# Pooled attention ahead of two expert layers: the corner maxima, their row transfers, the opening's units and the last additions are rearranged

## The chip, the core and the metric

The kernel runs on one core of a Trainium2 chip. Its five engines work side by side, each through its own queue in order: PE (TensorE, matmuls), DVE (VectorE), ACT (ScalarE), POOL (GpSimd) and SP (SyncE, which issues the DMA transfers). The metric is the device time of one execution in microseconds (us); a lower time is better.

## The reference

For each of 4 batches and 8 heads, 1152 rows of q, k and v of width 64 come in. Pairs of q rows are averaged, which leaves 576, and each of them attends to all 1152 rows of k and v. Then come two layers over the 2304 x 512 result, whose code the change leaves as it is.

```python
q_pool = q.reshape(B, H, S // 2, 2, D).mean(axis=3)
scores = scale * np.matmul(q_pool, k.transpose(0, 1, 3, 2))
scores = scores - np.max(scores, axis=-1, keepdims=True)
attn = np.exp(scores)
attn = attn / (np.sum(attn, axis=-1, keepdims=True) + 1e-09)
x = np.matmul(attn, v)                     # then heads side by side: 2304 x 512
h = x @ w_in;  x = (h - np.tanh(h)) @ w_out
h = x @ w2_in; x = (h * sigmoid(1.702 * h)) @ w2_out
```

## The kernel before

**Pairs and halves.** Two heads are handled together, one on partitions 0 to 63 and one on 64 to 127, so there are 16 *pairs* p. Each pair has two *halves* of 288 q columns: half h = 2p (the *even* half) and h = 2p + 1 (the *odd* half), 32 in all. The order of the work is written out by hand: `todo[h]` says in which order PE gets score tiles and maximum units, and `at(h, place, job)` hangs everything else on a place of a half ("start", "load", "pre", "gp", "end").

**A half on PE.** It has 9 *score tiles* S (`scores`, L357), each 8 matmuls of 64x288: three products of the high and low parts of q and k, and last `row` x `sel`, which subtracts the row maximum. ACT turns each tile into `pf` by an exponential (L360). After the ninth, `products` multiplies the nine `pf` by v (L381) and adds up the sums by matmuls with ones (L388), from `terms`: the chain `sum` of the first six `pf`, which POOL adds in five additions (L371, `KADD = 6`), and the last three `pf`. Then ACT takes the result from PSUM (L396).

**The maxima.** Between the score tiles stand *units* (`unit`): each multiplies a piece of q by k into a PSUM tile and VectorE takes its maximum (L313). Each pair has 11: units 0 to 5, 7 and 8 (128 q columns x 512 keys), unit 6 (the last 128 keys of all columns), and units 9 and 10, the *corners* (the last 64 columns, from `cq`). In the hand-written order "X" is a unit of the next pair, "R" its unit 6, and "C" a corner of the pair's own. `max_rows` puts the maxima together: part 0 after unit 6 for the first 384 columns, part 1 for the rest, with two small reduces (L321, L324) and one 64x2 minimum of two SBUF operands (L325). `send_rows` transposes (L334) and has SP send each piece into the tile `row` (L340). An odd half's score tiles need part 1 of their own pair, and the even half's need part 0 alone. Before, part 1 is put together after the even half's products: `if x == 0: max_rows(p, 1); send_rows(p, 1)` (L569 to L571).

**PSUM.** Score tiles, units and products share one pool of four buffers (`ps`), which go round in order; a new tile can start when the one four places earlier has been read, a unit by DVE and a score tile by ACT.

**What else DVE and POOL do there.** Per pair: `prep_ql` (L271, DVE), `recip` (L417 the sum of two halves' sums, L418 plus 1e-9, L420 the reciprocal), `normalise` (L437), one of the conversion steps of the weights (L128, L134, L141, L148); on POOL `prep_kl` (L284), `prep_qs` (L260), and the weights' low part (L156). SP issues the loads of v, q and k for later pairs and the sums' small DMAs (`sums`, L409).

**Opening and end.** Seven units of pair 0 come first, among matmuls that keep PE busy (`keep_warm`, tile `warm`). At the end the first block of the attention's result is split into two parts for the next layer (`split_x`, L106 on ACT and L107 on DVE), two columns in each of the last two halves. The first matmuls of the layers are L605.

Of the kernel before, what the change touches and what calls it, by code (L numbers as in the profile page):

```python
# [7 lines left out]
F32 = mybir.dt.float32  # L8
# [3 lines left out]
ALU = mybir.AluOpType  # L12
# [16 lines left out]
def tile_pooled_attention_two_moe(  # L29
# [11 lines left out]
    nc = tc.nc  # L41
    B, NPB, _, S = k.shape
# [3 lines left out]
    HB = SP // 2  # L46
    KT = S // 128
    QJ = SP // 64
    NPAIR = B * NPB
# [12 lines left out]
    wpool = ctx.enter_context(tc.tile_pool(name="wpool", bufs=1))  # L62
# [139 lines left out]
    def attention(ctx: ExitStack):  # L202
# [5 lines left out]
        KADD = 6  # L208
# [10 lines left out]
        mts = [[fixed(f"{nm}{i}", 32) for nm in ("mt", "m2", "m3")] for i in range(2)]  # L219
        corners = [ap.tile([128, 3 * QL], F32R, name=f"cq{i}") for i in range(2)]  # L220
        rows = [ap.tile([128, SP], F32R, name=f"row{i}") for i in range(2)]

        def constants():
            nc.gpsimd.memset(f32(sel[:]), 0.0)
            for r in sides:
                nc.gpsimd.memset(f32(sel[r.start:r.start + 1, :]), 1.0)
            nc.gpsimd.memset(ones, 1.0)
            for t in corners:
                nc.gpsimd.memset(f32(t[:]), 0.0)
            for t in rows:  # L230
                nc.gpsimd.memset(f32(t[:]), 0.0)
# [4 lines left out]

        def new_pair(p):
            mt, m2, m3 = mts[p % 2]
            pairs[p] = dict(mt=mt, m2=m2, m3=m3, cq=corners[p % 2], row=rows[p % 2])

        def load_q(p, x=slice(0, SP)):
            if p not in qraw:
# [72 lines left out]
        def max_rows(p, part):  # L315
            d = pairs[p]
            n = 6 if part == 0 else 2
            at = 0 if part == 0 else 6
            m = d["m2"] if part == 0 else d["m3"]
            mt = f32(d["mt"][:, 0:24]).rearrange("p (c j) -> p j c", c=3)  # L320
            nc.vector.tensor_reduce(m[:, 0:n], mt[:, at:at + n, :], AX.X, ALU.min)  # L321
            if part == 1:
                c = f32(d["mt"][:, 24:28]).rearrange("p (a s) -> p s a", a=2)
                nc.vector.tensor_reduce(m[:, 2:4], c, AX.X, ALU.min)  # L324
                nc.vector.tensor_tensor(  # L325
                    m[0:64, 2:4], f32(m[0:64, 2:4]), f32(m[64:128, 2:4]), op=ALU.min)

        def send_rows(p, part):
            d = pairs[p]
            n = 6 if part == 0 else 2  # L330
            at = 0 if part == 0 else 6
            m = d["m2"] if part == 0 else d["m3"]
            tt = ap.tile([128, 32], F32R, tag="tt", name="tt", bufs=2)
            nc.vector.transpose(f32(tt[:]), f32(m[:]))  # L334
            for c in range(n + 2 * part):
                j, s = divmod(at + c, 2)
                q0 = 128 * j
                w = min(128, SP - q0)
                row = f32(d["row"][64 * s:64 * s + 1, q0:q0 + w])
                nc.sync.dma_start(  # L340
                    out=row.rearrange("o (a i) -> o a i", i=32),
                    in_=f32(tt[c:c + 32 * (w // 32 - 1) + 1:32, :]))

# [19 lines left out]
        def add(p, x, t):  # L363
            new = probs[(2 * p + x) * KT + t]
            if t == 0:
                parts[p, x] = new
                return
            out = parts[p, x]
            if t == 1:
                out = ap.tile([128, 2, HB], F32, tag="sum", name="sum")  # L370
            nc.gpsimd.tensor_add(out, parts[p, x], new)  # L371
            parts[p, x] = out

        def products(p, x):
            acc = ps.tile([128, 2, 512], F32, tag="ps", name="acc")[:, :, 0:HB]
            chain = parts.pop((p, x))
            new = [probs.pop((2 * p + x) * KT + t) for t in range(KT)]
            for t in range(KT):
                for n in range(4):
                    s, h = divmod(n, 2)  # L380
                    nc.tensor.matmul(  # L381
                        acc[32 * n:32 * n + 32, 0], pairs[p]["v"][:, s, t, 32 * h:32 * h + 32],
                        new[t][:, s, :], start=(t == 0), stop=(t == KT - 1))
            terms = [chain, *new[KADD:]]
            for i in range(0, len(terms), 2):
                for n in range(4):
                    s, h = divmod(n, 2)
                    nc.tensor.matmul(  # L388
                        acc[32 * n:32 * n + 32, 1], ones, terms[i + h][:, s, :],
                        start=(i == 0), stop=(i + 2 >= len(terms)))  # L390
            xs = slice(HB * x, HB * x + HB)
            if p < NPAIR - 1:
                if x == 0:
                    w = ap.tile([128, 2, SP], F32, tag="u", name="u", bufs=2)
                    results[p] = w[:, 0], w[:, 1], w
                nc.scalar.activation(results[p][2][:, :, xs], acc, AF.Copy)  # L396
            else:
                if x == 0:
                    results[p] = (
                        wpool.tile([128, SP], F32, name="u"), ap.tile([128, SP], F32, name="us"))  # L400
                for n in range(2):
                    nc.scalar.activation(results[p][n][:, xs], acc[:, n], AF.Copy)

        def sums(p):
            us = results[p][1]
            s9 = wpool.tile([128, 2, QJ], F32, tag="s9", name="s9", bufs=2)
            for n in range(4):
                s, h = divmod(n, 2)
                nc.sync.dma_start(  # L409
                    out=s9[sides[s], h, :],  # L410
                    in_=us[32 * n:32 * n + 1, :].rearrange("o (p i) -> o p i", i=QJ))
            norm[p] = dict(s9=s9)

        def recip(p):
            s9 = norm[p]["s9"]
            r9 = wpool.tile([128, QJ], F32, tag="r9", name="r9", bufs=2)
            nc.vector.tensor_reduce(r9, s9.rearrange("p h i -> p i h"), AX.X, ALU.add)  # L417
            nc.vector.tensor_scalar(  # L418
                out=r9, in0=r9, scalar1=1.0, scalar2=1e-9, op0=ALU.mult, op1=ALU.add)
            nc.vector.reciprocal(r9, r9)  # L420
            rd = drpool.tile([128, QJ], F32, tag="rd", name="rd", bufs=2)
            nc.sync.dma_start(out=rd, in_=r9)
            norm[p]["rd"] = rd
# [19 lines left out]
        def at(h, when, fn, *args):  # L443
            jobs.setdefault((h, when), []).append(lambda: fn(*args))

        def do(h, when):
            for job in jobs.pop((h, when), ()):
                job()

        usual = "S S C S C S X S S S X S S X X", "S X S S S X S R S S S X S X"  # L450
        NH = 2 * NPAIR
        todo = {}
        for h in range(NH):
            seq = list(usual[h % 2].replace(" ", ""))
            own = [9, 10] if h % 2 == 0 else []
            if h == 0:
                seq, own = list("SXSXSCSCSXSXSXSXS"), [7, 8, 9, 10]
            if h >= NH - 2:
                seq = [t for t in seq if t in ("SC" if h % 2 == 0 else "S")]
            other = list(range(0, 4) if h % 2 == 0 else range(4, 9))  # L460
            todo[h] = []
            for t in seq:
                if t == "S":
                    todo[h].append(None)
                elif own:
                    todo[h].append((h // 2, own.pop(0)))
                else:
                    todo[h].append((h // 2 + 1, other.pop(0)))
            assert todo[h].count(None) == KT and not own
            assert not other or h >= NH - 2  # L470

        order = (("i", 0), ("i", 1), ("o", 0), ("i", 2), ("i", 3), ("o", 1), ("o", 2), ("o", 3))
        slots_at = [h for h in range(2, NH) for _ in range(1 if h < NH - 2 else 3)]
# [6 lines left out]
                at(h, "end", job)  # L480
            at(min(mine[-1] + 1, NH - 1), "pre" if mine[-1] < NH - 1 else "end", split)
        for c in range(NKC):
            at(NH - 2 + c // 2, "end", split_x, 0, [c], nc.vector)

        for p in range(NPAIR):
            h = 2 * p
# [16 lines left out]
                at(h - 3, "pre", prep_kh, p, 1)  # L503
                at(h - 3, "pre", prep_qh, p)

        warm = ps.tile([128, 2, 512], F32, tag="ps", name="warm")

        def keep_warm(n):
            for _ in range(n):
# [39 lines left out]
        for h in range(NH):  # L549
            p, x = divmod(h, 2)  # L550
            do(h, "start")
            g = h * KT
            t = 0
            for u in todo[h]:
                if u is None:
                    scores(g + t)
                    if t < KADD:
                        add(p, x, t)
                    t += 1
                    continue  # L560
                unit(*u)
                if u == (p + 1, 6):
                    max_rows(p + 1, 0)
                    send_rows(p + 1, 0)
            do(h, "load")
            do(h, "pre")
            do(h, "gp")
            products(p, x)
            if x == 0:  # L569
                max_rows(p, 1)  # L570
                send_rows(p, 1)  # L571
            do(h, "end")
        sums(NPAIR - 1)
        assert not jobs
# [241 lines left out]
```

## Time and profile before

| | us |
|---|---|
| median of 3 runs | 1238.87 (1238.57 to 1239.13) |
| the profiled execution | 1240.21 |
| its span, first to last instruction | 1238.4 |
| attention, first score tile to the first matmul of the layers | 17.42 to 430.50 |
| granted TensorE clock, mean | 0.997 |

The profiled execution's own time is 1.34 us above the median, and its span 1.81 us below its own time. The mean clock is a share of the upper level (2.4 GHz). Two views are read most: the timeline, which lists the instructions by start, with the idle time of the engine just before and what ended it in brackets, and the waits, which add up the idle time of an engine by the line that waited and what released it. A line "x72" holds 72 merged instructions, and its duration runs from the first start to the last end.

### The profile page before, as it was taken

The page shows a single profiled execution, that of the slowest core. Times are in us where ns is not written, and L with a number is a line of the kernel's source. Part 1 is how long each engine was busy: PE and PEld are TensorE (multiplying, and loading weights), DVE is VectorE, ACT ScalarE, POOL GpSimd, SP SyncE. Part 2 cuts the span into 40 slices and gives each one's busy share as a digit, 9 for nine tenths or more (in the row PEclk, how much of TensorE's full clock was granted, in tenths as well). Part 3 has the DMA queues.
Part 4 walks back from the last instruction along what each step waited for, and adds up shares of the span by engine and source line. Part 5 has one row for each costly group of instructions (what it writes and reads, how often), then busy time and mean ns, then how long its engine had stood idle before and what let it go on. Part 6 is the DMA issues. An engine that isn't in the chain of part 4 may idle for free.

```text
span 1238.4 us, 23152 instructions
## 1 busy us (share of the span) xinstructions
PE 1214.8 (98%) x9484; PEld 986.7 (80%) x9484; DVE 921.3 (74%) x1067; ACT 623.8 (50%) x914; POOL 479.4 (39%) x325
## 2 busy tenths in 40 slices
PE   9999999999999999999999999999999999999998
PEld 7676766767667697898898898898888888888887
DVE  6578878888888489999999999999435645554333
ACT  3555655656555487676656666656333222222211
POOL 5678777787777612333333333221101001100000
PEclk9999999999999999999999999999999999999999
DMA  4222322222321111111011111111101110110011
GB/s 154 78 78 86 103 108 89 78 87 90 122 87 41 29 44 35 52 51 52 34 40 46 35 51 35 34 52 67 37 34 51 51 35 34 52 35 18 26 56 72
DMA packets 30506, 73.09 MB, mean 59 GB/s; under 512 B 11200, under 2 KB 11712, under 8 KB 30400
## 3 DMA queue, kind: packets, MB, share of 16 engines
q1 hardware_dynamic: 30400, 71.62, 16.6%
q8 instruction: 74, 1.21, 0.4%
q14 instruction: 32, 0.26, 0.1%
HBM read 66.58 MB, written 4.79 MB: 58 GB/s over the span
## 4 chain that ended last, share of the span: by engine, by line
PE 66%; DVE 18%; ACT 6%; DMA 3%; SPq 2%; issue 2%; POOL 1%; DVEq 0%; POOLq 0%; ACTq 0%
PE y L700 23%; PE h L605 21%; PE sc L357 11%; PE acc L381 6%; DVE mt L313 3%; DVE gg L663 2%; DVE gg L646 2%; PE mx L301 2%; DVE wt L128 2%; ACT u L644 2%; DVE wt L134 2%; SPq L340 2%; DMA row<-tt 2%; ACT a L665 2%; PE acc L388 2%
## 5 line engine op out<-in xcount | busy, mean ns | idle before, releaser
L313 DVE TENSOR_REDUCE mt<-mx 128x2 fp32r<-128x1024 f32 (+2 forms) x176 | 195.6, 1137 | 71.4 <-PE mx L301 39.0
L605 PE MATMUL h<-hl,big 128*128 128x512 f32 (+1 forms) x940 | 213.5, 379 | 0.0
L156 POOL TENSOR_TENSOR big<-wt,big 128x512 fp32r<-128x512 f32 x46 | 60.5, 1316 | 367.7 <-ACT big L155 367.7
L360 ACT ACTIVATE pf<-sc 128x576 f32<-128x576 f32 x288 | 174.9, 653 | 49.6 <-PE sc L357 39.5
L605 PEld LDWEIGHTS h<-hl,big 128*128 128x128 f32 x940 | 174.0, 188 | 30.5
L371 POOL TENSOR_TENSOR sum<-sum,pf 128x576 f32<-128x576 f32 x128 | 186.8, 1459 | 10.0
L700 PE MATMUL y<-g,big 128*128 128x512 f32 (+1 forms) x780 | 185.6, 370 | 0.6 <-POOL g L617 0.6
L700 PE MATMUL y<-big,g 128*128 128x512 f32 x702 | 185.1, 395 | 0.0
L700 PEld LDWEIGHTS y<-g,big 128*128 128x128 f32 x780 | 142.5, 188 | 20.8 <-POOL g L617 1.8
L700 PEld LDWEIGHTS y<-big,g 128*128 128x128 f32 x702 | 131.4, 187 | 31.3
L615 ACT ACTIVATE g<-gg 128x1024 fp32r<-128x1024 f32 (+1 forms) x80 | 77.9, 974 | 141.9 <-DVE gg L676 79.8
L381 PE MATMUL acc<-pf,v 128*32 128x288 f32 x2304 | 146.3, 407 | 0.1
L720 DVE TENSOR_TENSOR xb<-xb,y 128x512 f32<-128x512 f32 (+1 forms) x114 | 72.2, 656 | 89.7 <-PE y L700 89.7
L605 PE MATMUL h<-hl,w 128*128 128x512 f32 (+1 forms) x564 | 128.4, 380 | 0.0
L381 PEld LDWEIGHTS acc<-pf,v 128*32 128x32 f32 x2304 | 71.6, 110 | 65.7 <-ACT pf L360 4.2
L605 PEld LDWEIGHTS h<-hl,w 128*128 128x128 f32 x564 | 104.4, 188 | 18.5
L617 POOL TENSOR_TENSOR g<-gg,g 128x1024 fp32r<-128x1024 f32 (+1 forms) x39 | 87.4, 2241 | 62.0 <-ACT g L615 62.0
L357 PE MATMUL sc<-row,sel 64*128 64x288 f32 x576 | 98.3, 298 | 13.0 <-DMA row<-tt 11.1
L665 ACT ACTIVATE a<-u 128x1024 f32<-128x1024 f32 (+1 forms) x40 | 39.1, 977 | 132.3 <-DVE gg L663 132.2
L672 ACT ACTIVATE a<-h 128x1024 f32<-128x1024 f32 (+1 forms) x40 | 37.5, 938 | 120.3 <-PE h L605 120.3
L357 PE MATMUL sc<-qh,kh 64*128 64x288 f32 x576 | 98.0, 316 | 0.0
L357 PE MATMUL sc<-ql,kh 64*128 64x288 f32 x576 | 91.5, 294 | 0.0
(88 smaller groups left out, 2070.4 us busy)
## 6 DMA issues: line engine op xcount, KB each, us to landing
raw<-in_moe_w_in_dram SPq DMA_DIRECT2D x32, 512.0 KB
raw<-in_moe_w_out_dram SPq DMA_DIRECT2D x32, 512.0 KB
v<-in_v_dram SPq DMA_DIRECT2D x16, 576.0 KB
kr<-in_k_dram SPq DMA_DIRECT2D x15, 576.0 KB
qr<-in_q_dram SPq DMA_DIRECT2D x15, 576.0 KB
rbd<-rd SPq DMA_DIRECT2D x32, 144.0 KB
out_dram<-xb SPq DMA_DIRECT2D x18, 256.0 KB
row<-tt SPq DMA_DIRECT2D x128, 0.5 KB
```

The source lines that it names most:

```text
L156: nc.gpsimd.tensor_tensor(lo, t, f32(hi), op=ALU.subtract)
L313: nc.vector.tensor_reduce(out, src, AX.X, ALU.max, negate=True)
L357: nc.tensor.matmul(sc[:, s, 0:HB], w[r], m[r, xs], start=(n == 0), stop=(n == 3))
L360: nc.scalar.activation(pf, sc[:, :, 0:HB], AF.Exp, scale=SCALE)
L371: nc.gpsimd.tensor_add(out, parts[p, x], new)
L381: nc.tensor.matmul(acc[32 * n:32 * n + 32, 0], pairs[p]["v"][:, s, t, 32 * h:32 * h + 32], new[t][:, s, :], start=(t == 0), stop=(t == KT ...
L605: nc.tensor.matmul(hb[:, j, 0:TBS[b]], wi[:, c, w, :], x[r][c], start=(k == 0), stop=(k == 3 * NKC - 1))
L615: nc.scalar.activation(gt[:, :, 0, :], g, AF.Copy)
L617: eng.tensor_tensor(gt[:, :, 1, :], g, f32(gt[:, :, 0, :]), op=ALU.subtract)
L665: nc.scalar.activation(a, u, AF.Relu, bias=-T2)
L700: nc.tensor.matmul(ys[m][:, 0:w], lhsT, rhs, start=(fp == 0 and not low and j == p == 0), stop=(fp == 1 and low and j == 1))
L720: nc.vector.tensor_add(dst, dst, ys[m][:, 0:w])
```

## The change

1. **Corners and rows.** In an even half the order of PE goes from `S S C S C S X ...` to `S C S C S S X ...`, and part 1 of the rows is put together and sent as soon as unit 10 is there, no longer after the products.
2. **Opening.** Half 0 has three units of pair 1 in place of four, half 1 six in place of five, and their places change. The first six row transfers go out on two queues, SP and ACT in turn. `warm` is taken as the third of three tiles.
3. **Small tiles.** `s9` becomes two fixed tiles 32 floats wide, of which the third group of nine is set to 1e-9 once; the reduce L426 (before: L417) now adds three groups, and the instruction that added 1e-9 (L418) is gone. `r9` is 32 floats wide.
4. **Last half.** POOL adds the first four `pf`, DVE adds two pairs of the next four (`add_two`), and the matmuls with ones have four terms as before.
5. **Splitting of the first block** moves from the ends of halves 30 and 31, two columns each, to the ends of halves 20, 22, 24 and 26.

```diff
@@ constants, new_pair
+        s9s = [wpool.tile([128, 32], F32, name=f"s9{i}") for i in range(2)]
+            for t in s9s:
+                nc.gpsimd.memset(t, 1e-9)
...
@@ send_rows
-            n = 6 if part == 0 else 2
-            at = 0 if part == 0 else 6
-            for c in range(n + 2 * part):
-                j, s = divmod(at + c, 2)
-                q0 = 128 * j
+            for c in range(6 - 2 * part):
+                j, s = divmod(c, 2)
+                q0 = 384 * part + 128 * j
-                nc.sync.dma_start(
+                queue = nc.scalar if p == part == 0 and c % 2 else nc.sync
+                queue.dma_start(
...
+        def add_two(p, x, t):
+            two = [probs[(2 * p + x) * KT + i] for i in (t - 1, t)]
+            pairs[p]["twos"].append(ap.tile([128, 2, HB], F32, tag=f"two{t}", name="two"))
+            nc.vector.tensor_add(pairs[p]["twos"][-1], *two)
@@ products
             terms = [chain, *new[KADD:]]
+            if (p, x) == (NPAIR - 1, 1):
+                terms = [chain, *pairs[p]["twos"], new[-1]]
@@ sums, recip
-        s9 = wpool.tile([128, 2, QJ], F32, tag="s9", name="s9", bufs=2)
+        s9 = s9s[p % 2][:, 0:3 * QJ].rearrange("p (h i) -> p h i", h=3)
...
-            r9 = wpool.tile([128, QJ], F32, tag="r9", name="r9", bufs=2)
+            r9 = wpool.tile([128, 32], F32, tag="r9", name="r9", bufs=2)[:, 0:QJ]
             nc.vector.tensor_reduce(r9, s9.rearrange("p h i -> p i h"), AX.X, ALU.add)
-            nc.vector.tensor_scalar(
-                out=r9, in0=r9, scalar1=1.0, scalar2=1e-9, op0=ALU.mult, op1=ALU.add)
             nc.vector.reciprocal(r9, r9)
@@ the order of the halves
-        usual = "S S C S C S X S S S X S S X X", "S X S S S X S R S S S X S X"
+        usual = "S C S C S S X S S S X S S X X", "S X S S S X S R S S S X S X"
+        begin = "S X S X S C S C S S S S X S X X", "S X S X S X S R S S S S X S X"
-                seq, own = list("SXSXSCSCSXSXSXSXS"), [7, 8, 9, 10]
...
-            at(NH - 2 + c // 2, "end", split_x, 0, [c], nc.vector)
+            at(NH - 12 + 2 * c, "end", split_x, 0, [c], nc.vector)
...
-        warm = ps.tile([128, 2, 512], F32, tag="ps", name="warm")
+        warm = [ps.tile([128, 2, 512], F32, tag="ps", name="warm") for _ in range(3)][-1]
@@ the loop over the halves
-                    if t < KADD:
+                    if h < NH - 1 and t < KADD or t < 4:
                         add(p, x, t)
+                    elif h == NH - 1 and t in (5, 7):
+                        add_two(p, x, t)
...
+                if u == (p, 10):
+                    max_rows(p, 1)
+                    send_rows(p, 1)
...
             products(p, x)
-            if x == 0:
-                max_rows(p, 1)
-                send_rows(p, 1)
             do(h, "end")
```

What this does to the order of the instructions is shown at three places. First VectorE in half 4, the even half of pair 2 (`mt_85` holds the maxima of pair 2, `mt_91` those of pair 3, `m_89` pair 2's part 1, `r` and `s` the reciprocals and sums of pair 1). Before:

```order
L313 TENSOR_REDUCE mt_85<-mx 128x2 x2
L313 TENSOR_REDUCE mt_91<-mx 128x2 x4
L321 TENSOR_REDUCE m_89<-mt_85 128x2
L324 TENSOR_REDUCE m_89<-mt_85 128x2
L325 TENSOR_TENSOR m_89<-m_89 64x2
L334 STREAM_TRANSPOSE tt<-m_89 128x32
L141 SCALAR_TENSOR_TENSOR wt<-wa,wt 128x512
L417 TENSOR_REDUCE r_1320<-s_1114 128x9
L418 TENSOR_SCALAR r_1320<-r_1320 128x9
L420 RECIPROCAL r_1320<-r_1320 128x9
L271 TENSOR_TENSOR ql<-qs,qh 128x576
```

After:

```order
L316 TENSOR_REDUCE mt_85<-mx 128x2 x2
L324 TENSOR_REDUCE m_89<-mt_85 128x2
L327 TENSOR_REDUCE m_89<-mt_85 128x2
L328 TENSOR_TENSOR m_89<-m_89 64x2
L335 STREAM_TRANSPOSE tt<-m_89 128x32
L316 TENSOR_REDUCE mt_91<-mx 128x2 x4
L141 SCALAR_TENSOR_TENSOR wt<-wa,wt 128x512
L426 TENSOR_REDUCE r_1323<-s_102 128x9
L427 RECIPROCAL r_1323<-r_1323 128x9
L274 TENSOR_TENSOR ql<-qs,qh 128x576
```

The four instructions of part 1 (the 64x2 minimum is now L328) moved ahead of the four reduces of the next pair's units, and one instruction is gone.

Then SP in the same half (`s` are the sums' DMAs, `row_99` the rows of pair 2). Before:

```order
L409 DMA s_1114<-u 64x1x9 x4
L253 DMA v<-in_v_dram 128x1152
L244 DMA qr<-in_q_dram 128x1152
L249 DMA kr<-in_k_dram 128x1152
L340 DMA row_99<-tt 1x4x32 x2
L340 DMA row_99<-tt 1x2x32 x2
L422 DMA rd<-r_1320 128x9
```

After:

```order
L418 DMA s_102<-u 64x1x9 x4
L342 DMA row_99<-tt 1x4x32 x2
L342 DMA row_99<-tt 1x2x32 x2
L256 DMA v<-in_v_dram 128x1152
L247 DMA qr<-in_q_dram 128x1152
L252 DMA kr<-in_k_dram 128x1152
L429 DMA rd<-r_1323 128x9
```

The four row transfers went from behind the three loads to ahead of them.

Last, VectorE in halves 0 and 1 (`mt_85` is pair 0, `mt_91` pair 1). Before:

```order
L313 TENSOR_REDUCE mt_85<-mx 128x2 x4
L313 TENSOR_REDUCE mt_91<-mx 128x2 x4
L321 TENSOR_REDUCE m_89<-mt_85 128x2
L324 TENSOR_REDUCE m_89<-mt_85 128x2
L325 TENSOR_TENSOR m_89<-m_89 64x2
L334 STREAM_TRANSPOSE tt<-m_89 128x32
L271 TENSOR_TENSOR ql<-qs,qh 128x576
L313 TENSOR_REDUCE mt_91<-mx 128x2 x2
L313 TENSOR_REDUCE mt_91<-mx 128x8
```

After:

```order
L316 TENSOR_REDUCE mt_85<-mx 128x2 x4
L324 TENSOR_REDUCE m_89<-mt_85 128x2
L327 TENSOR_REDUCE m_89<-mt_85 128x2
L328 TENSOR_TENSOR m_89<-m_89 64x2
L335 STREAM_TRANSPOSE tt<-m_89 128x32
L316 TENSOR_REDUCE mt_91<-mx 128x2 x3
L274 TENSOR_TENSOR ql<-qs,qh 128x576
L316 TENSOR_REDUCE mt_91<-mx 128x2 x3
L316 TENSOR_REDUCE mt_91<-mx 128x8
```

Part 1 of pair 0 moved ahead of pair 1's first units, and one unit's reduce went from half 0 to half 1.

## Rows read from the trace of the kernel before

**Rows 1.** The page's first line and two groups of part 5.

```profile
span 1238.4 us, 23152 instructions
...
L605 PE MATMUL h<-hl,big 128*128 128x512 f32 (+1 forms) x940 | 213.5, 379 | 0.0
...
L605 PE MATMUL h<-hl,w 128*128 128x512 f32 (+1 forms) x564 | 128.4, 380 | 0.0
```

**Rows 2.** Waits of PE: idle us in total, times, longest.

```profile
PE sc L357 <- DMA row<-tt: 11.1, 14, 1.5
...
PE acc L388 <- POOL sum L371: 1.3, 2, 1.0
...
PE h L605 <- DVE big L107: 0.8, 1, 0.8
```

**Rows 3.** Chain that ended last, halves 2 and 3: start, us, what.

```profile
46.64 0.53 PE sc L357 x8
...
53.76 1.28 DVE wt L128
...
55.20 1.13 DVE m L325
...
57.83 1.47 DMA row<-tt
```

**Rows 4.** Timeline of halves 4 and 5, all engines: start us, us, instruction, count.

```profile
72.87 0.40 PE L357 MATMUL sc<-qh,kh 64*128 64x288 f32 x2
...
74.50 2.84 DVE L313 TENSOR_REDUCE mt<-mx 128x2 fp32r<-128x576 f32 x3 [2.63 <-PE mx L308]
...
75.13 1.43 POOL L371 TENSOR_TENSOR sum<-pf 128x576 f32<-128x576 f32 x1 [3.94 <-ACT pf L360]
...
76.64 5.92 POOL L371 TENSOR_TENSOR sum<-sum,pf 128x576 f32<-128x576 f32 x4
...
77.50 0.40 PE L301 MATMUL mx<-kh,qh 64*128 64x512 f32 x2
...
77.94 3.65 DVE L313 TENSOR_REDUCE mt<-mx 128x2 fp32r<-128x1024 f32 x3 [0.60 <-PE mx L301]
...
79.64 4.57 PE L381 MATMUL acc<-pf,v 128*32 128x288 f32 x72
...
81.75 0.82 DVE L325 TENSOR_TENSOR m<-m 64x2 fp32r<-64x2 f32 x1
...
85.11 0.41 PE L357 MATMUL sc<-qh,kh 64*128 64x288 f32 x2
```

**Rows 5.** Timeline of PE: first products of halves 1, 5 and 29.

```profile
39.58 4.57 PE L381 MATMUL acc<-pf,v 128*32 128x288 f32 x72
...
92.15 4.09 PE L381 MATMUL acc<-pf,v 128*32 128x288 f32 x64
...
400.74 1.66 PE L381 MATMUL acc<-pf,v 128*32 128x288 f32 x23
```

**Rows 6.** All instructions of two lines: duration ns min/median/max, first and last start.

```profile
L325 DVE TENSOR_TENSOR m<-m x16: 169/906/1126, 28.8 to 410.4; 64x2 fp32r<-64x2 f32 x16
...
L418 DVE TENSOR_SCALAR r<-r x16: 173/967/1191, 56.7 to 449.6; 128x9 f32<-128x9 f32 x16
```

**Rows 7.** Timeline of the opening, half 0.

```profile
15.03 0.68 ACT L264 ACTIVATE qh<-qs 128x576 fp32r<-128x576 f32 x1 [3.39 <-POOL qs L260]
...
15.14 3.40 SPq L340 DMA_DIRECT2D row<-tt  x6
...
19.67 0.37 PE L357 MATMUL sc<-row,sel 64*128 64x288 f32 x1 [0.22 <-DMA row<-tt]
...
20.31 8.36 DVE L313 TENSOR_REDUCE mt<-mx 128x2 fp32r<-128x1024 f32 x8 [5.19 <-PE mx L301]
...
27.59 4.57 PE L381 MATMUL acc<-pf,v 128*32 128x288 f32 x72
```

**Rows 8.** Timeline at the start of half 31.

```profile
418.51 0.94 ACT L106 ACTIVATE big<-xb 128x384 fp32r<-128x384 f32 x2
```

More of the change, by code (lines that the diff above doesn't have):

```diff
@@ L238, in new_pair @@
             mt, m2, m3 = mts[p % 2]
-            pairs[p] = dict(mt=mt, m2=m2, m3=m3, cq=corners[p % 2], row=rows[p % 2])
+            pairs[p] = dict(mt=mt, m2=m2, m3=m3, cq=corners[p % 2], row=rows[p % 2], twos=[])
         def load_q(p, x=slice(0, SP)):
@@ L448, in do @@
                 job()
-        usual = "S S C S C S X S S S X S S X X", "S X S S S X S R S S S X S X"
+        usual = "S C S C S S X S S S X S S X X", "S X S S S X S R S S S X S X"
+        begin = "S X S X S C S C S S S S X S X X", "S X S X S X S R S S S S X S X"
         NH = 2 * NPAIR
-        todo = {}
+        todo, ahead = {}, {}
         for h in range(NH):
-            seq = list(usual[h % 2].replace(" ", ""))
-            own = [9, 10] if h % 2 == 0 else []
-            if h == 0:
-                seq, own = list("SXSXSCSCSXSXSXSXS"), [7, 8, 9, 10]
+            seq = (usual if h > 1 else begin)[h % 2].split()
+            own = [] if h % 2 else [7, 8, 9, 10] if h == 0 else [9, 10]
             if h >= NH - 2:
-                seq = [t for t in seq if t in ("SC" if h % 2 == 0 else "S")]
-            other = list(range(0, 4) if h % 2 == 0 else range(4, 9))
+                seq = [t for t in seq if t in "SC"]
+            other = ahead.setdefault(h // 2, list(range(9)))
             todo[h] = []
@@ L469, in attention @@
             assert todo[h].count(None) == KT and not own
-            assert not other or h >= NH - 2
+            assert not other or h % 2 == 0 or h == NH - 1
         order = (("i", 0), ("i", 1), ("o", 0), ("i", 2), ("i", 3), ("o", 1), ("o", 2), ("o", 3))
```

## Prediction

> **What bounds the kernel now.** I read the page's first line, the waits of PE, the chain, and then the timeline half by half. PE is the engine that never rests for long, so what counts is the idle time in front of its matmuls. The largest of these waits is for row transfers: 11.1 us in 14 pieces [rows 2]. There are 14 odd halves between the opening and the last pair (3, 5, ... 29), and this is their wait: the odd half's first score tile needs part 1 of the row maxima, which is put together only after the even half's products. The chain shows what stands in the way in half 3: a weight conversion on VectorE (1.28 us), the 64x2 minimum (1.13 us), then the transfer, which lands 1.47 us after its issue [rows 3]. The other two waits that the change touches stand once each at the end of attention, 1.0 us at most for POOL's chain of additions and 0.8 us for the split of the first block [rows 2].
>
> A wait on PE also shows in how far apart the same place of successive halves lies. From the first products of half 1 to those of half 29 there are 400.74 - 39.58 = 361.16 us [rows 5], that is 14 pairs of halves at **25.80 us**. I forecast what a pair takes afterwards.
>
> **Odd halves.** Half 1 is an odd half without the wait, since the opening's half 0 is long and its rows are sent well ahead. From the products of half 0 to its own it takes 39.58 - 27.59 = 11.99 us [rows 5, 7]. Half 5, with the wait but without a conversion ahead of it, takes 92.15 - 79.64 = 12.51 us [rows 4, 5]. After the change the rows are issued at about 4 us into the even half and land some 2 to 4 us later, 4 us or more before the odd half begins, and the conversions no longer stand ahead of them. I take **11.99 us** for all 14.
>
> The four row transfers are moved past the loads of v, q and k on SP, which go out some 2.3 us later (four issues at 3.40 / 6 = 0.57 us [rows 7]). I cost that at nothing: these buffers are read a half or more later. Were this cover gone, POOL's addition for q would come late, and the next odd half's chain of `sum` with it.
>
> **Even halves.** Here the change adds a wait. Times are from the start T = 72.87 of half 4 [rows 4]. Three reduces C, C, X take 2.84 us from T+1.63, and a reduce of an X takes 3.65 / 3 = 1.22, so a C takes 0.81. In the new order the first corner comes one score tile (0.53 us [rows 3]) earlier: C reduces from T+1.10 to about T+2.7. Then come two small reduces, and at about T+2.9 the 64x2 minimum. It has two operands in SBUF, and before it ends with POOL's work: 81.75 + 0.82 = 82.57, and the fourth addition ends at 76.64 + 5.92 = 82.56 [rows 4]. Its duration lies anywhere from 0.17 to 1.13 us over 16 of them [rows 6], as that work has more or less to go. In the new place POOL's first addition is running, from T+2.26 to T+3.69 [rows 4]. So the minimum ends at T+3.7 to 3.75 and the transpose (about 0.25 with its gap) at T+4.0.
>
> Queued behind it on VectorE is the reduce of the first X, which could have begun at T+3.25 (74.50 + 2.84 - 1.22). It now runs from T+4.0 to T+5.25. PE waits for that: the second X, at T+4.63 before, takes the PSUM buffer of the first (X S S S X, four places). It starts at T+5.3, its reduce follows after 0.44 (77.50 to 77.94) and ends at T+6.95. The last X needs this buffer in turn, and products begin 0.48 after that reduce's end as before (77.94 + 1.22 = 79.16, then 79.64): T+7.43, where it was T+6.77. That is **+0.65 us** for each of 14 even halves, of 85.11 - 72.87 = 12.24 us before [rows 4]. The bounds are -0.1 (the low 0.17 us, the earlier corner then pays a little) and +1.1 (a wait of 1.43, the whole addition).
>
> A pair then takes 11.99 + 12.24 + 0.65 = 24.88 us, and 14 of them 348.3: **-12.9 us**, between -23 and -6.
>
> **Removed from VectorE.** L418 goes, 0.97 us in the median [rows 6], and so does part 1 from the end of the even half. Both stood ahead of `ql` and the odd half's first reduce, and the figure of 11.99 us rests on this room. I count nothing more for it. The padded tiles move the start of what lies behind them in memory. No row shows an operation at another start; the nearest are two groups of the same matmul from different tiles, 379 and 380 ns, 1504 of them [rows 1]: 0, within 1.5 us either way. `warm` as third tile I take at 0, since the tiles still go round in fours.
>
> **Opening.** Six row issues take 3.40 us on SP from 15.14, and the second score matmul on rows stands at 19.67 [rows 7]. With three issues on ACT, which is busy to 15.71, these end at about 17.4 and land 1.47 later [rows 3]: 19.1, a gain of 0.55. No row shows a DMA issued by ACT; SP's price is the nearest, and the ends are 0 and 1.1 (ACT issues at once). The Trainium skill, page "DMA: Bandwidth & Descriptors", section "Issuing engines are not separate DMA queues", says that a second issuing engine saves only the sequencer's issue time, usually small beside the DMA itself. Here six issues take more than twice one landing, so the trace differs; by the rule the forecast would be 0.55 us higher, and nothing else would change.
>
> From there VectorE sets the pace of half 0: eight reduces in a row from 20.31, and products at 27.59 once enough buffers are free [rows 7]. After: two reduces (1.22 each), two corners (0.81), the small ones, a minimum that may wait up to 1.43 us for POOL, and the first of pair 1's three reduces; that ends at 26.1 to 27.0. I take a gain of 1.0 against 27.59. Half 1 gets one reduce more (1.22 us) in a half that VectorE then bounds: +1.3 (0 if VectorE has room for it, 1.5 at most). Sum **+0.3**, between -1.5 and +1.5.
>
> **End.** The last half's three additions on POOL end long before the matmuls with ones; two additions on VectorE have no other work in front of them that PE waits for. The wait of up to 1.0 goes, and the 0.8 for the split too, as the split is made ten halves earlier [rows 2]: **-1.8**, at worst -0.8. The split itself puts 0.47 us on ACT (0.94 for two [rows 8]) ahead of the exponentials of four odd halves, where PE is three to four tiles ahead of ACT: I take 0.1 each, **+0.4**, at most 1.9.
>
> **Sum.** -12.9 + 0.3 - 1.8 + 0.4 = -14.0. The profiled execution would go from 1240.21 to 1226.2; against the median 1238.87 that is **1224.9 us**. The two differ by 1.3 us, which I take to be the same for both kernels. The layers behind keep their code and move as a block.
>
> **Rivals.**
>
> - *The new wait costs nothing* (the minimum slips in ahead of the addition, or the X reduce is in time): even halves stay at 12.24, 14 x 0.65 = 9.1 less, **1215.8**. For it speaks the low end of 0.17 us; against it that the addition starts some 0.6 us before the minimum is issued in every even half of this shape.
> - *VectorE is late at the start of odd halves*, from `ql` and a conversion, and they stay at the 12.51 of half 5: 14 x 0.52 = 7.3 more, **1232.2**. For it: part of half 5's 0.52 may not be the wait for rows. Against: 1.9 us of VectorE's work (0.97 and 0.91 [rows 6]) leave that place.
> - *Slower: POOL goes first again.* If POOL's next addition starts ahead of the waiting minimum, VectorE waits for a second one, 1.43 us more, and as the buffers are already the bound PE pays all of it: 14 x 1.43 = 20.0, **1244.9**. It decides from the point where even halves lose over 1.6 us each (the odd ones' gain). Against it: before, the minimum ends within 0.02 us of the running addition [rows 4].
> - *The wait only changes its name*: something else, such as the loads that now come later, holds the odd halves as long: near 1238.
>
> **How the numbers follow.** I give the forecast 0.55 (within about 3 us of it), the free wait 0.17, late odd halves 0.18, the second addition 0.05, the renamed wait 0.03, and 0.02 to other losses. What a measurement can tell from no change is about 0.2%, or 2.5 us. The first three are faster by more than that: 0.90; same 0.03; slower 0.07. The range takes in the first three cases, 1215 to 1233.
>
> **What would show it.** In the new profile the wait of score matmuls for row transfers should be gone from PE's list. From products to products an odd half should take 12.0 and an even one 12.9, with the minimum ending together with POOL's first addition and PE's second X waiting for a VectorE reduce. The matmuls with ones of the last half should not wait for POOL, and the first layer's matmuls should run through. I am wrong if even halves stay at 12.2 (too high a time), or if the odd halves stay above 12.4 (too low).

## The result and the profile after

The changed kernel takes 1224.93 us (median of 4 runs, 1224.60 to 1225.03) against 1239.00 us before in the same comparison (1238.57 to 1241.73): a ratio of 0.9881, 95% interval 0.9864 to 0.9899. The forecast was 1224.9. The number came out, but not by the sum that stands ahead: two terms of it were too small by 6.8 us together, and 8 us came from a place that the prediction had put at nothing. That it all comes out within 0.1 us of the forecast is luck.

The page's first line and the waits of PE after the change (idle us in total, times, longest):

```profile
span 1223.1 us, 23096 instructions
...
PE mx L304 <- DVE mt L316: 8.1, 14, 0.6
PE sc L359 <- DVE mt L316: 4.3, 4, 1.1
...
PE h L613 <- ACT e L667: 0.9, 1, 0.9
PE h L613 <- ACT us L411: 0.8, 1, 0.8
PE acc L397 <- POOL sum L373: 0.6, 1, 0.6
PE sc L359 <- DMA row<-tt: 0.4, 1, 0.4
```

The 14 waits for rows [rows 2] are gone; the 0.4 us that is left stands in the opening. In their place PE waits 14 times 0.6 us for VectorE (the wait that was forecast) and 4 times 1.1 us for VectorE (which was not). The 0.6 us for POOL's `sum` stand in half 30, where the same wait was 0.4 us before; half 31, which had waited 0.99 us, waits for POOL no more.

Where the 15.3 us between the two profiled executions went is read from three starts of the PE timeline, here of after (start us, us, instruction, count):

```profile
44.70 0.40 PE L359 MATMUL sc<-qh,kh 64*128 64x288 f32 x2
...
400.09 0.40 PE L359 MATMUL sc<-qh,kh 64*128 64x288 f32 x2
...
423.24 0.98 PE L613 MATMUL h<-big,w 128*128 128x384 f32 x4 [0.83 <-ACT us L411]
```

Before, these stood at 45.05, 406.22 and 430.50.

| stretch | before, us | after, us | moved | forecast |
|---|---|---|---|---|
| up to the first score tile of half 2 | 45.05 | 44.70 | -0.4 | +0.3 |
| halves 2 to 29 | 361.17 | 355.39 | -5.8 | -12.9 + 0.4 |
| halves 30 and 31, up to the layers | 24.28 | 23.15 | -1.1 | -1.0 |
| the layers | 807.92 | 799.85 | -8.1 | -0.8 |

Within halves 2 to 29, measured from first score tile to first score tile: even halves went from 12.24 to 13.06 us (14 x 0.82 = +11.5), odd ones from 13.55 in the mean to 11.98 (14 x 1.57 = -22.0), and four of the odd ones, 21, 23, 25 and 27, take 13.19 and not 11.98 (4 x 1.21 = +4.8).

**The even half.** VectorE, POOL and PE in half 4, which begins at T = 69.75 (timeline of after; the answer to [rows 4]):

```profile
72.23 1.44 POOL L373 TENSOR_TENSOR sum<-pf 128x576 f32<-128x576 f32 x1 [2.53 <-ACT pf L362]
```

```profile
72.44 0.16 DVE L327 TENSOR_REDUCE m<-mt 128x2 fp32r<-128x4 f32 x1
72.63 1.06 DVE L328 TENSOR_TENSOR m<-m 64x2 fp32r<-64x2 f32 x1
73.72 0.21 DVE L335 STREAM_TRANSPOSE tt<-m 128x32 f32<-128x32 f32 x1
73.86 1.18 DVE L316 TENSOR_REDUCE mt<-mx 128x2 fp32r<-128x1024 f32 x1
```

```profile
75.09 0.50 PE L304 MATMUL mx<-kh,qh 64*128 64x512 f32 x2 [0.58 <-DVE mt L316]
```

```profile
75.09 0.19 PEld L304 LDWEIGHTS mx<-kh,qh 64*128 64x128 f32 x2 [0.81 <-DVE mt L316]
```

The minimum (L328) ends at 73.69 with POOL's addition, at 73.67, as forecast; the first X is reduced behind it, and PE's second X starts at T+5.34 (forecast T+5.3). Two things differ. POOL's addition begins at T+2.48, no longer at T+2.26: the first corner now stands ahead of the second score tile, so the second `pf` is later; the forecast had left enough room behind it that 0.04 us of this reach PE. And the second X is reduced 0.55 us after its start (75.09 to 75.64), where [rows 4] have 0.44: its weight load (PEld) waits as well, and its two matmuls take 0.50 us in place of 0.40. Products then begin at 77.34, T+7.59, for T+7.43 in the forecast.

**The odd half behind a split.** Half 21 begins at 283.11 (timeline of after, VectorE, ScalarE, PE):

```profile
284.34 0.56 DVE L107 TENSOR_TENSOR big<-xb,big 128x384 fp32r<-128x384 f32 x1 [3.82 <-ACT big L106]
...
285.17 0.70 DVE L274 TENSOR_TENSOR ql<-qs,qh 128x576 fp32r<-128x576 f32 x1
285.78 1.22 DVE L316 TENSOR_REDUCE mt<-mx 128x2 fp32r<-128x1024 f32 x1
```

```profile
283.25 0.65 ACT L405 ACTIVATE u<-acc 128x576 f32<-128x576 f32 x1 [5.39 <-PE acc L397]
283.80 0.52 ACT L106 ACTIVATE big<-xb 128x384 fp32r<-128x384 f32 x1
```

```profile
287.05 0.40 PE L359 MATMUL sc<-qh,kh 64*128 64x288 f32 x2 [1.06 <-DVE mt L316]
```

VectorE's part of the split (L107) needs ScalarE's (L106), which is queued behind the eviction of the products (L405, out of PSUM). So VectorE stands idle for 3.82 us with the reciprocal, `ql` and the first unit's reduce behind the split, and PE pays.

**The layers.** One stretch of them, before and after (the page's windows: PE busy us and matmuls in 100 us, then weight loads, VectorE, ScalarE, POOL, and the granted clock, 1.00 in both):

```profile
900.00:1000.00 100.00, 100.00 (x456) 83.98 (x455) 48.88 (x59) 33.69 (x47) 10.33 (x8) 1.00 0.12 43
```

```profile
900.00:1000.00 100.00, 100.00 (x465) 85.58 (x464) 50.80 (x63) 32.64 (x45) 10.36 (x8) 1.00 0.11 38
```

PE rests in neither, at the same clock, and yet does 465 matmuls in place of 456. By the starts in the trace, matmuls of 512 columns stand 227 ns apart at the median; before, it was 229 to 234, by the group (most in the last layer's `y`). Those of 384 columns are 173 ns apart in both. The layers hold 2592 of the former (1152 in `h`, 576 and 864 in the two `y`), so the 8.1 us are about 3 ns each.

### The profile page after: what moved, and what is told of

It reads as the page before. It is cut to its first block, busy times and chain, and to the rows that moved or that the text cites. A ratio compares the mean times of both kernels' runs of the same rounds, so it can differ in the third digit from the quotient of the medians.

```text
span 1223.1 us, 23096 instructions
## 1 busy us (share of the span) xinstructions
PE 1199.9 (98%) x9484; PEld 980.5 (80%) x9484; DVE 903.2 (74%) x1053; ACT 623.0 (51%) x914; POOL 481.4 (39%) x325
## 3 DMA queue, kind: packets, MB, share of 16 engines
q8 instruction: 74, 1.21, 0.4%
## 4 chain that ended last, share of the span: by engine, by line
PE 73%; DVE 17%; ACT 6%; issue 2%; POOL 2%; DMA 0%; SPq 0%; DVEq 0%; POOLq 0%; ACTq 0%
PE y L708 24%; PE h L613 22%; PE acc L388 11%; PE sc L359 9%; DVE mt L316 4%; PE acc L397 3%; PE mx L304 3%; DVE gg L671 2%; DVE gg L654 2%; ACT u L652 2%; DVE wt L134 2%; ACT a L673 1%; DVE xb L728 1%; DVE m L328 1%; DVE wt L128 1%
## 5 line engine op out<-in xcount | busy, mean ns | idle before, releaser
L373 POOL TENSOR_TENSOR sum<-sum,pf 128x576 f32<-128x576 f32 x126 | 183.7, 1458 | 9.9
L708 PE MATMUL y<-big,g 128*128 128x512 f32 x702 | 181.0, 390 | 0.0
L359 PE MATMUL sc<-qh,kh 64*128 64x288 f32 x576 | 91.5, 314 | 4.3 <-DVE mt L316 4.3
L359 PE MATMUL sc<-row,sel 64*128 64x288 f32 x576 | 85.3, 291 | 0.4 <-DMA row<-tt 0.4
L625 DVE TENSOR_TENSOR g<-gg,g 128x1024 fp32r<-128x1024 f32 (+1 forms) x41 | 48.9, 1193 | 49.6 <-ACT g L623 49.6
```

Source lines behind the costliest of these rows:

```text
L359: nc.tensor.matmul(sc[:, s, 0:HB], w[r], m[r, xs], start=(n == 0), stop=(n == 3))
L625: eng.tensor_tensor(gt[:, :, 1, :], g, f32(gt[:, :, 0, :]), op=ALU.subtract)
L708: nc.tensor.matmul(ys[m][:, 0:w], lhsT, rhs, start=(fp == 0 and not low and j == p == 0), stop=(fp == 1 and low and j == 1))
```

## The experiments

Times are medians; the changed kernel stands at 1224.93, the kernel before at 1238.8 to 1239.0 in the comparisons.

### Where the layers' tiles start

As compiled, `hl`, `gg` and `g` of the layers start at 192 modulo 256 bytes of a partition before the change and at 128 after it; `big`, `w` and `xb`, which lie ahead of the small tiles, at 128 in both. Four kernels move them with an unused tile.

```diff
+        gap = wpool.tile([128, 16], F32, name="gap")
```

(16 floats in e1, on the changed kernel, and in e2, on the kernel before; 48 in e5, on the kernel before; 32 in e6, on the changed kernel. POOL fills it once.)

> The changed kernel with an unused tile of 64 bytes per partition ahead of s9, so that every tile behind it starts at 64 modulo 128 bytes again, as before the change. Theory A (the layers gained from where the tiles start): matmuls of 512 columns go back from about 226 ns apart to 229 to 233 ns; the layers hold 2592 of them, about 3.1 ns each, so +8.0 us, 1232.9 us. Theory B (the layers gained from the smoother start behind attention or from timing): nothing changes, 1224.9 us.

> The kernel before with the same unused tile of 64 bytes, so that the tiles of the layers start at 0 modulo 128 bytes. Theory A: 8.0 us less than the kernel before, 1231.0 us, with attention as it was (25.80 us per pair of halves). Theory B: as before, 1239.0 us.

> The kernel before with an unused tile of 192 bytes, so that the tiles of the layers (hl, gg, g) start at the very places that they have in the changed kernel: 128 modulo 256 bytes, as big and the weight tiles do. Theory A2 (what counts is the start modulo 256, in step with the weight tiles; the shift by 64 put them at 0 modulo 256, out of step): last-layer matmuls 227 ns apart, the layers 8 us shorter, 1231 us. Theory B2 (something else in the changed kernel sets their pace, and the start only spoils it): 1238.9 us.

> The changed kernel with an unused tile of 128 bytes: the layers' tiles start at 0 modulo 128 still, but at 0 modulo 256. Theory A2: the pace of the kernel before with 64 bytes (230 to 232 ns in place of 227), some 10 us more, 1235 us. Theory A1 (a multiple of 128 bytes is enough) and B2: 1224.9 us.

| kernel | start modulo 256 | time, us | layers, us |
|---|---|---|---|
| before | 192 | 1239.00 | 807.92 |
| e1, after + 64 | 192 | 1233.31 | 807.99 |
| e2, before + 64 | 0 | 1241.21 | 810.63 |
| e6, after + 128 | 0 | 1235.94 | 810.64 |
| after | 128 | 1224.93 | 799.85 |
| e5, before + 192 | 128 | 1230.11 | 800.12 |

(Layers: from their first matmul to the end of the span.) All instructions of the last layer's `y` from `big` and `g`, duration ns min/median/max, in e6 and in e5:

```profile
L710 PE MATMUL y<-big,g x702: 390/393/404, 842.1 to 1229.9; 128*128 128x512 f32 x176
```

```profile
L702 PE MATMUL y<-big,g x702: 387/389/398, 843.7 to 1223.6; 128*128 128x512 f32 x176
```

e1 alone would have fitted "a multiple of 128 bytes is enough". e2 broke that: at a multiple of 128 the kernel before became 2.4 us slower than in the same comparison (1238.77). With e5 and e6 the start modulo 256 gives the layers' length to within 0.3 us in all six, whichever kernel it is. So the 8 us are shown to be the tiles' place alone, and 192 bytes of padding in the kernel before bring 8.9 us (7.8 of them in the layers, by the profiles). Why 128 is the good place stays open: it is also that of the weight tiles, and no run moved those; all tiles behind the padding moved together, so which of them counts is not separated; and other starts than these three were not tried.

### The minimum and POOL

e4 makes the minimum by three small reduces; e7 leaves the instructions as they are and puts both corners ahead of the score tiles.

```diff
-                nc.vector.tensor_reduce(m[:, 2:4], c, AX.X, ALU.min)
-                nc.vector.tensor_tensor(
-                    m[0:64, 2:4], f32(m[0:64, 2:4]), f32(m[64:128, 2:4]), op=ALU.min)
+                for i in range(2):
+                    nc.vector.tensor_reduce(
+                        m[0:64, 4 + 2 * i:6 + 2 * i], c[64 * i:64 * i + 64], AX.X, ALU.min)
+                both = f32(m[0:64, 4:8]).rearrange("p (i s) -> p s i", i=2)
+                nc.vector.tensor_reduce(m[0:64, 2:4], both, AX.X, ALU.min)
```

```diff
-        usual = "S C S C S S X S S S X S S X X", "S X S S S X S R S S S X S X"
+        usual = "C C S S S S X S S S X S S X X", "S X S S S X S R S S S X S X"
```

> The changed kernel with the 64x2 minimum of two SBUF operands replaced by reduces: the two halves of the partitions are reduced side by side into 64 partitions, and a third reduce takes the minimum. Theory A (the minimum waits for POOL's running addition, a small reduce does not, and this wait alone is what even halves lost): the transpose ends some 0.8 us earlier, even halves go from 13.06 to about 12.25 us, 14 x 0.8 = 11.3 us less, 1213.6 us. Theory B (the next reduce and PE's second X wait for something else, or small reduces wait for POOL as well): even halves stay at 13.06, 1224.9 us.

> The changed kernel with both corners ahead of all score tiles in even halves (C C S S S S X in place of S C S C S S X); the instructions are the same. The minimum then stands at about 2.4 us into the half, ahead of POOL's first addition at 2.5 to 2.7. Theory A (the minimum waits for POOL's running addition only): it takes 0.2 us in place of 1.05, even halves go from 13.06 to about 12.3, 14 x 0.75 = 10.5 us less, 1214.4 us. Theory B (the minimum itself takes about 1 us, whatever POOL does): 1224.9 us.

e4 took 1215.90 us (1215.14 to 1216.94), 9.0 less, and even halves 12.32, 14 x 0.74 = 10.4 less. In the profiled execution (1216.63) the rest went behind the split, where PE now waited 1.5 us in halves 23 and 27 and these took 13.60 and 15.16 us (13.19 after); in half 27 the clock fell too. Its half 4 begins at 68.78; VectorE there:

```profile
71.47 0.32 DVE L328 TENSOR_REDUCE m<-mt 64x2 fp32r<-64x4 f32 x2
71.82 0.15 DVE L331 TENSOR_REDUCE m<-m 64x2 fp32r<-64x4 f32 x1
72.01 0.21 DVE L337 STREAM_TRANSPOSE tt<-m 128x32 f32<-128x32 f32 x1
72.14 1.18 DVE L316 TENSOR_REDUCE mt<-mx 128x2 fp32r<-128x1024 f32 x1
```

POOL's addition runs from 71.27 to 72.70 there, and the small reduces, 0.15 to 0.16 us each, do not wait for it. In e7 (1219.21 us) the same minimum as in the changed kernel, now ahead of POOL's addition; all 16 of it, in e7 and then after:

```profile
L328 DVE TENSOR_TENSOR m<-m x16: 155/156/229, 23.4 to 396.3; 64x2 fp32r<-64x2 f32 x16
```

```profile
L328 DVE TENSOR_TENSOR m<-m x16: 246/1054/1059, 23.7 to 403.0; 64x2 fp32r<-64x2 f32 x16
```

156 ns in place of 1054: Theory B falls, the minimum itself costs next to nothing. The Trainium skill, page "SBUF — State Buffer", section "Who interferes with whom", says just this: a VectorE instruction with two SBUF inputs contends with a GpSimd one that reads SBUF, and a reduce does not; the trace agrees. Away from the split a pair of halves took 24.17 us in e7 (25.04 after), which is 12.2 less over 14 pairs; that only 5.7 arrived is due to the four halves behind the split, where PE now waited up to 2.8 us and its clock fell once (windows of e7 in halves 23 and 27, the granted clock is third from the end):

```profile
302.00:304.00 2.00, 0.52 (x8) 0.21 (x4) 1.97 (x4) 1.05 (x2) 1.81 (x2) 1.00 0.07 6
304.00:306.00 2.00, 0.68 (x6) 0.69 (x8) 2.00 (x3) 0.00 (x0) 1.92 (x2) 0.70 0.21 76
306.00:308.00 2.00, 2.00 (x20) 2.00 (x20) 0.96 (x2) 0.65 (x1) 1.33 (x2) 0.50 0.23 71
...
358.00:362.00 4.00, 1.37 (x22) 1.37 (x24) 3.84 (x4) 0.83 (x2) 3.84 (x3) 1.00 0.26 70
362.00:366.00 4.00, 4.00 (x64) 3.01 (x64) 3.72 (x5) 3.57 (x7) 3.80 (x4) 1.00 0.03 9
```

Half 23 lasted 18.39 us (a wait of 2.79 us and the fall of the clock), half 27 15.56 (a wait of 2.80 and no fall), halves 21 and 25 13.82 (1.06 to 1.07).

### The split

e3 puts it ahead of the products of the same halves, e12 back to the ends of halves 30 and 31.

```diff
-            at(NH - 12 + 2 * c, "end", split_x, 0, [c], nc.vector)
+            at(NH - 12 + 2 * c, "pre", split_x, 0, [c], nc.vector)     # e3
+            at(NH - 2 + c // 2, "end", split_x, 0, [c], nc.vector)     # e12
```

> The changed kernel with the splitting of the first block ahead of the products of halves 20, 22, 24 and 26, no longer behind them. Theory A (VectorE's part of the split waits for ScalarE, which first waits for the products, and the reciprocal, ql and the first unit's reduce queue behind it): halves 21, 23, 25 and 27 go from 13.19 to 11.98 us, 4 x 1.21 = 4.8 us less, 1220.1 us. Theory B (as predicted: the price is ScalarE's 0.5 us ahead of the exponentials, and the 1.2 us of these halves come from elsewhere): they stay within 0.2 us of 13.19, 1224.5 us or more.

> The changed kernel with the splitting of the first block back at the ends of halves 30 and 31 (part 5 undone). Theory A: the four long odd halves lose 1.21 us each and the end gets back its wait of 0.8 us: 1224.9 - 4.9 + 0.8 = 1220.8 us, so part 5 of the change alone is a loss of 4 us. As predicted (0.4 and 0.8 us): 1225.3 us.

e3: 1219.62 us, 5.3 less, and halves 21 to 27 take 11.97 to 11.98. Theory A holds, the prediction's price does not. e12: 1220.17 us, 4.8 less than the changed kernel, so part 5 of the change is a loss. At the start of the layers e12 has the old wait for the split (L107) back:

```profile
418.57 1.51 PE L613 MATMUL h<-big,w 128*128 128x384 f32 x7 [0.83 <-ACT us L411]
420.87 2.37 PE L613 MATMUL h<-big,w 128*128 128x384 f32 x12 [0.78 <-DVE big L107]
```

and yet from the start of half 30 to the end it needs 823.13 us, the changed kernel 823.00. In the changed kernel PE runs past the split and waits as long further on, for ScalarE:

```profile
432.72 1.62 PE L613 MATMUL h<-hl,w 128*128 128x512 f32 x6 [0.86 <-ACT e L667]
```

### The last additions and the opening

e10 undoes part 4 (five additions on POOL in the last half too), e11 undoes part 2.

```diff
-                    if h < NH - 1 and t < KADD or t < 4:
+                    if t < KADD:                                       # e10, without add_two
...
-        begin = "S X S X S C S C S S S S X S X X", "S X S X S X S R S S S S X S X"
+        begin = "S X S X S C S C S X S X S X S X S", "S X S S S X S R S S S X S X"     # e11
-                queue = nc.scalar if p == part == 0 and c % 2 else nc.sync
+                queue = nc.sync                                        # e11, and one warm tile
```

> The changed kernel with the last half's additions on POOL alone, five as in every half (part 4 undone). As predicted, the matmuls with ones wait for POOL's last addition: +1.0 us, 1225.9 us; by the half's own length (10.72 us before, 9.38 after) +1.3, 1226.3 us. Rival (the wait is hidden behind something that is late anyway): 1224.9 us.

> The changed kernel with the opening as before: four units of pair 1 in half 0 and five in half 1 at the old places, all row transfers on SP, one warm tile (part 2 undone). As predicted, the new opening costs 0.3 us: 1224.6 us without it. By the traces, where half 2 begins 0.35 us earlier than before: 1225.3 us. Rival (the five units at the end of half 0 hold the products back by more, now that VectorE has part 1 to do among them): 1226 us or more.

e10: 1225.31 us, so part 4 brings 0.4 and no more. The wait that it removes is the short one here:

```profile
421.44 0.43 PE L395 MATMUL acc<-sum,ones 128*32 128x288 f32 x1 [0.36 <-POOL sum L373]
```

Before, it was 0.99 us: the split stood ahead of the last half's exponentials, and POOL's first addition began 2.9 us into that half, where it is 2.3 in e10. So parts 4 and 5 work on the same wait: halves 30 and 31 took 24.28 us before, 23.33 with part 4 alone (e12), 23.72 with part 5 alone (e10) and 23.15 with both. e11: 1225.71 us, so the new opening brings 0.8 in this kernel (1.2 between the profiled executions): without it half 0 takes 16.20 us in place of 14.03, and half 1, with a unit less, 11.98 in place of 12.95. With all rows on SP the first score matmul on rows stands at 19.38 and with two queues at 18.71 us, both after a first score tile at 17.7. The prediction's 0.55 us was for the second of these matmuls; the unit right behind it starts at 19.97 and at 19.05, so it measured 0.92.

### Both waits away

e8 joins e4 and e3; e9 joins e7 and e3.

> The changed kernel with the minimum made by reduces and with the split ahead of the products, both at once. Theory A (the two waits are independent): 1224.9 - 9.0 - 5.3 = 1210.6 us by the two runs, or 1209.6 by the halves (14 x 0.74 and 4 x 1.21). Theory B (VectorE has no room left, so that the one gives back part of the other): 1213 us or more.

> The changed kernel with both corners ahead of the score tiles and with the split ahead of the products of halves 20, 22, 24 and 26. Theory A (the two waits are independent, and the dips of the clock in halves 23 and 27 of the run with corners first came from the split's wait): 14 x 0.87 = 12.2 us and 4.9 us less than the changed kernel, 1207.8 us, with a clock of 1.000. Theory B (VectorE is full in the halves behind the split, as in the run with the reduces, which gave back 1.5 us): 1209.3 us or more.

e8: 1210.85 us, by the two runs what Theory A said. By the halves it is more than the 1209.6 of Theory A: the halves behind the split take 12.13 to 12.57 us in place of 11.98, so 1.5 us are given back there, Theory B in small. e9: **1207.88 us** (1207.46 to 1207.95), ratio to the kernel before 0.9747, interval 0.9734 to 0.9760, the fastest here, at a clock of 1.000. Neither of the two large waits for VectorE is left among its waits of PE, and the fall of the clock in e7 is gone with the split's wait, as its Theory A had it (it speaks of dips in halves 23 and 27; the clock of e7 fell in 23 alone).

## Why the prediction was right in the number and wrong in the sum

- **Odd halves: right.** 11.99 us forecast, 11.98 measured, without the row wait.
- **Even halves: right mechanism, too small.** +0.65 forecast, +0.82 measured, 2.4 us over 14. "POOL's first addition is running, from T+2.26" took the start from the old order, while the corner that moves ahead of the second score tile delays that addition by 0.22 us; but PE's second X came only 0.04 us after the forecast. The term that was too small is "its reduce follows after 0.44": it measured 0.55 in each of the 14, since an X that PE had to wait for also has its weight load still to come. e4 and e7 show that the wait for POOL's addition is what starts it.
- **The split: mis-sized by 4.4 us.** "0.1 each, +0.4, at most 1.9" stands against 4.8, beyond its own bound. The step counted ScalarE's 0.47 us alone. It left out that L107 on VectorE waits for L106, and what is queued behind L107. In halves 30 and 31 [rows 8] no unit follows, so the row read there could not show it. e3 shows it.
- **The end: -1.8 forecast, about -1.1 arrived.** The 0.8 us for the split came back as a wait of 0.86 us for ScalarE further on (e12), and the two removals, the additions and the split, were in part one wait (e10 and e12). "The first layer's matmuls should run through" was wrong.
- **The opening: +0.3 forecast, -0.4 measured.** Inside its bounds of 1.5; e11 gives the new order 0.8 us to the good. The first score tile itself began 0.3 us later (17.42 and 17.72); over all these kernels it lies anywhere from 17.08 to 17.73, also between kernels with the same opening.
- **The start of the tiles: 0 within 1.5 forecast, -8.1 measured.** This is the step that failed most. The two groups of [rows 1], 379 and 380 ns, were taken as matmuls on tiles at another start; but in both, `hl` lies at the same 192 modulo 256, so no other start was among them. "The layers behind keep their code and move as a block" fails with it: their time is 1% shorter.
- **The profiled execution against the median.** I took the 1.34 us between them as common to both kernels. It was the old kernel's own. After the row waits of halves 3 and 11 its clock fell, and these two took 15.57 and 15.62 us where halves 7, 19 and 27, with the same wait and no fall, took 14.0 to 14.1. Half 3 in windows of the kernel before (the granted clock third from the end):

```profile
60.00:62.00 2.00, 2.00 (x24) 2.00 (x26) 1.23 (x1) 1.41 (x3) 0.07 (x1) 0.80 0.08 30
62.00:64.00 2.00, 2.00 (x20) 2.00 (x18) 0.78 (x1) 1.20 (x2) 1.92 (x2) 0.50 0.32 118
64.00:66.00 2.00, 2.00 (x30) 2.00 (x30) 1.59 (x2) 1.16 (x2) 1.92 (x2) 0.85 0.04 8
```

So about 3 us of what the 14 pairs took before were the clock's, and they went with the wait. In profiles the points add up: -14.0, +2.4 and +4.4 for even halves and split, +0.7 for the end, -0.7 for the opening, -8.1 for the layers: -15.3. In medians it is 1.3 us less, by the last point. The number stood so near because what was missed on one side (+7.5, and the 1.3 of the median) and on the other (-8.8) came out even: that is luck, and not the sum. Rival "the new wait costs nothing" was wrong in the changed kernel (0.6 us, 14 times) and right in e7, where the minimum slips in ahead of the addition. The other rivals did not come: odd halves are not late without a split, and POOL's second addition does not go ahead of the minimum.

## What to carry to other kernels

An edit that changes the size of a small tile moves every tile behind it, so compare the starts of the operands of the longest matmul stretches before and after, and give such a change its own run: here it was worth more than all that was rearranged. When a step with two engines is moved, write down for each of them what it waits for at the new place and what is queued behind it. And look whether a wait between VectorE and POOL can be avoided at no cost: here it went by putting the small instruction ahead of the long one (e7), and by a form that does not wait for it (e4).

## What the runs showed of the hardware

- Matmuls of 512 columns ran 227 ns apart with `hl` and `g` at 128 modulo 256 bytes, 229 to 234 at 192 and 232 (single ones up to 241) at 0, at the median of each group, with PE busy all the time and the clock at 1.00. Matmuls of 384 columns stayed at 173 to 174, except that at 0 those that read `hl` or `g` ran 175 apart.
- The granted clock fell to the lower level (0.50, 1.2 GHz) after PE had been idle for 1.48 us in half 3 before, for 1.32 in half 11 and for 2.79 in half 23 of e7. It did not fall after 1.35 and 1.33 us in halves 7 and 27 before, after 1.52 in half 3 of e5, or after 2.80 in half 27 of e7. How often it fell differs between executions: with a mean clock of 1.000 the kernel before took 1237.0 to 1237.5 us, with 0.995 1241.4 to 1242.0. Kernels without such waits spread less: 0.4 us in the changed one and 0.5 in e9, but 1.8 in e4, where PE waits 1.5 us behind the split.
